# Transnormer attention and a four-expert mixture on one core: neighbouring chunks of experts 1 to 3 share two of seven up products as 256-row matmuls, down products are scaled where they lie, and the norm's factors are kept in 4 KB rows

## The chip, the cores and the metric

One Trainium2 chip, one of its cores. The time is the device time of one execution in microseconds (us). Each kernel is run several times; of the kernel before three runs are shown. A profile is one further execution, recorded by the hardware profiler.

## What is computed

The reference is an attention without softmax followed by a mixture of four experts, all in fp32:

```python
kv = np.einsum('bhsd,bhse->bhde', k, v)            # q, k, v: (8, 8, 576, 64)
out = np.einsum('bhsd,bhde->bhse', q, kv)
rms = np.sqrt(np.mean(out * out, axis=-1, keepdims=True) + 1e-06)
x = (out / rms * g_norm).transpose(0, 2, 1, 3).reshape(4608, 512)
p = domain_probs / (domain_probs.sum(-1, keepdims=True) + 1e-09)
for e in range(4):                                  # w1[e]: 512x1024, w2[e]: 1024x512
    h = np.maximum(x @ w1[e], 0.0)
    out += p[:, e:e + 1] * (h @ w2[e])
```

## The kernel before

**Tiling.** The 4608 tokens are cut into nine chunks of 512: one for each of the eight batches, and a ninth of the 64 tokens that each batch of 576 has left. The program takes the experts one after the other and, in each, all nine chunks; step `s` is expert `s // 9`, place `s % 9`. While expert 0 works on a chunk, `attention` (L1121) makes the x of the next batch. Chunks' x factors are kept in DRAM and loaded again for experts 1 to 3 (`x_again`, L1476).

**Products.** Both matrix products are done by a seven-product (Strassen-like) scheme in two levels. For the up product of a chunk there are seven outer products, taken in the order `OUTER` = (1, 2, 6, 5, 3, 7, 4), and in each of them seven inner ones, in the order `ORDER` = (1, 6, 2, 5, 7, 4, 3). One inner product of `up` (L1514) is 2 x 2 matmuls: two quarters `u` of the weights by two halves of 64 columns (`halves_of`, L581, line L585), which go to different halves of the array. A matmul is 128x64 weights by 128 moving rows of x. It shows as two records in the trace (the kernel's own `pe`, L578, counts two passes), so that an inner product is 8 records. The results lie in PSUM banks `u1`, `u2`. ScalarE (ACT) copies the result of inner product 1 into another bank as a seed, on which product 2 accumulates; it copies those of 6 and 7 to `snap` tiles, and 2 and 4 to the result tile (L1563). VectorE (DVE) adds the results of 7 and 3 to the snaps (L1571). That is five copies and two sums of 256 columns for each outer product. Sums of whole outer products follow, 128x1024 each, on DVE or GpSimd (POOL) (`combine`, L608), and ReLUs on ACT (L1527).

**Down.** `down_deep` (L1819) does the same for the down product of chunks from step 7 on, with 128 moving rows and two outer products side by side in one bank. Its results are added up (L1944), scaled by the token's probability on ACT into a separate accumulator tile (`merge`, L1716), and sent as four blocks of 128 tokens by 512 columns. Expert 0 stores them by SyncE's queue (SP), later experts add them into the output in DRAM by an accumulating DMA on POOL's queue (`send`, L1732, issued at L1740). The last chunk (`down`, L1753) loads the sum back and finishes on the core.

**The norm.** In `attention` the squares are summed on the PE, and the inverse roots of batch `b`, 64 heads-by-tokens rows of 160, are written to DRAM (`roots`, L1297) and read back broadcast over 64 partitions each (`spread`, L1306: 512 bytes a piece, two DMAs of 256 KB for each half of the chunk; `spread_left`, L1313). DVE multiplies them in (L1322, L1329) and so makes the chunk's x, from which matmuls read directly.

**What sets the order.** Nothing is written in program order. Every step adds operations with a key (the place in PE's order), an estimated cost by engine, buffers and dependencies; `Plan` (L44) is a list scheduler that plays the whole kernel through at build time and writes out one fixed order for each engine. An engine takes the operation with the earliest due time among those that are ready; SP takes the first that is ready. Kinds of buffers (`big`, 31 tiles of 128x1024; `snap`; `xf`, the five places for x factors; the PSUM banks) have a fixed number of slots and are handed out in that order. `DEALS` (L72) lists for some steps the random draws that shift due times. So any edit can move instructions everywhere; only semaphores hold at run time.

Of the kernel before, what the change touches and what calls it, by code (L numbers as in the profile page):

```python
# [43 lines left out]
class Plan:  # L44
# [410 lines left out]
def kernel(  # L455
# [68 lines left out]
        "big": (31, 2 * NT), "w1y": (7, 768), "xa": (1, 4 * NT), "xb": (1, 4 * NT),  # L524
        "w2e": (1, 2 * NT), "snap": (5, HN),
# [8 lines left out]
    for kind, n in BANKS.items():  # L534
# [16 lines left out]
    slots["w2y"] = [w2y_home[:, i, :] for i in range(3)]  # L551
    halved = slots["db"]
# [4 lines left out]
        ((kind,), "xf", [slots[kind][0][:, i * 2 * NT:(i + 1) * 2 * NT] for i in range(n)])  # L557
        for kind, n in (("xa", 2), ("xb", 2), ("w2e", 1))
# [14 lines left out]
        b: dram.tile([D, P + 32], F32, tag=f"roots{b}", name=f"roots{b}") for b in range(1, B)  # L573
# [119 lines left out]
    TAIL = (1, 6, 5, 7)  # L693
    GROUPS = ((1, 7), (6, 5), (4,))
# [426 lines left out]
    def attention(b, key, span, rem):  # L1121
# [160 lines left out]
        def invert(eng):  # L1282
# [11 lines left out]
        sent, kept_roots = Buf(None, f"root{b}"), roots[b]  # L1294
        plan.add(
            when, SPC,
            lambda eng: nc.sync.dma_start(out=kept_roots[:], in_=both[0].ap[0:P:2, 0:wide]),  # L1297
            reads=both[:1], writes=[sent], kb=41, lands=2.6,
        )
        for s, (qt, tokens, mine) in enumerate(done):  # L1300
            xh = x_halves(b)[s]

            def spread(eng, xh=xh, s=s):
                rows = kept_roots[:].rearrange("(n i s r) t -> r s i n t", i=2, s=2, r=2)
                for r in range(2):
                    nc.sync.dma_start(  # L1306
                        out=xh.ap[r * D:(r + 1) * D, :].rearrange("p (n t) -> p n t", t=P),
                        in_=rows[r, s, 0, :, 0:P].unsqueeze(0).to_broadcast([D, 8, P]))

            def spread_left(eng, s=s, mine=mine):  # L1310
                rows = kept_roots[:].rearrange("(j i s r) t -> r s i j t", i=4, s=2, r=2)
                for r in range(2):
                    nc.sync.dma_start(  # L1313
                        out=xs.ap[r * D:(r + 1) * D, mine].rearrange("p (j t) -> p j t", j=NR),
# [897 lines left out]
```

## Time and profile before

| | |
|---|---|
| median of 3 runs | 1631.18 us (1630.81 to 1631.45) |
| the profiled execution, its own time | 1631.92 us |
| its span in the trace | 1630.1 us |
| granted TensorE clock | 1.00 |
| PE / DVE / ACT / POOL busy | 1622.5 / 1337.2 / 986.9 / 612.9 us |
| moved by DMA | 241.02 MB, mean 148 GB/s |

The span leaves 1.8 us of the execution's own time outside. PE, PEld, DVE, ACT and POOL are the tensor engine's matmuls and weight loads, VectorE, ScalarE and GpSimd; SPq is SyncE, which only issues DMAs. A row of a view by lines names the line of the kernel, the engine, the operation, the tile written and the tiles read, the count, the busy time and the mean duration in ns. A row of the windows gives for a stretch of time the busy us and in brackets the number of instructions of each engine. Matmuls are pipelined: the duration of one record is a latency, and its price is the distance from start to start.

### The profile page before, as it was taken

The numbers are of one execution on the slowest core, as the hardware profiler recorded it, in microseconds if no ns is written. First come the engines' busy times: TensorE is split into PE (matmuls) and PEld (weight loads), VectorE is DVE, ScalarE is ACT, GpSimd is POOL, SyncE is SP. The second block draws the span as 40 slices with busy tenths as digits, with TensorE's granted clock in tenths as the row PEclk, the third lists the DMA queues.
The fourth block names the chain that finished last, engine by engine and source line by source line (L and its number), as shares of the span: only waits on it lengthen the run. The fifth ranks groups of instructions, "written<-read, shape, count | busy, mean of one in ns | idle before, by whom it ended". The sixth has DMA issues, their size and how long they took to land.

```text
span 1630.1 us, 66925 instructions
## 1 busy us (share of the span) xinstructions
PE 1622.5 (100%) x29082; PEld 1564.6 (96%) x29082; DVE 1337.2 (82%) x2188; ACT 986.9 (61%) x2504; POOL 612.9 (38%) x597
## 2 busy tenths in 40 slices
PE   9999999999999999999999999999999999999999
PEld 5788999989999999999999999999999999999998
DVE  5788888889888888878988888887788987777776
ACT  4456655665566666666666666666566666566563
POOL 4233432323443443344344533332344443332232
PEclk9999999999999999999999999999999999999999
DMA  9877787855664435444676454444478544444442
GB/s 242 217 190 204 204 216 194 213 166 205 183 176 125 118 93 156 119 111 113 175 190 144 107 133 114 108 111 111 131 183 184 131 107 117 118 107 117 118 106 53
DMA packets 229312, 241.02 MB, mean 148 GB/s; under 512 B 101047, under 2 KB 172542, under 8 KB 229018
## 3 DMA queue, kind: packets, MB, share of 16 engines
q1 hardware_dynamic: 205402, 199.96, 40.9%
q0 software_dynamic: 23616, 36.78, 15.2%
q8 instruction: 228, 3.74, 1.0%
q14 instruction: 66, 0.54, 0.1%
HBM read 162.21 MB, written 74.47 MB: 145 GB/s over the span
## 4 chain that ended last, share of the span: by engine, by line
PE 98%; DVE 1%; DMA 1%; ACT 0%; issue 0%; SPq 0%; DVEq 0%; ACTq 0%
PE u L585 48%; PE db L585 31%; PE ab L585 16%; PE ab L1193 1%; PE ab L1218 0%; PE ab L1261 0%; PE ab L2156 0%; PE db L1218 0%; DVE big L608 0%; DMA kv<-in_v_dram 0%; DMA out_dram<-big 0%; SPq L2079 0%; PE u L997 0%; DMA small<-in_q_dram 0%; DVE small L608 0%
## 5 line engine op out<-in xcount | busy, mean ns | idle before, releaser
L608 DVE TENSOR_TENSOR big<-big,big 128x1024 f32<-128x1024 f32 (+1 forms) x612 | 547.6, 913 | 32.3 <-ACT big L1527 14.1
L585 PE MATMUL db<-big,big 128*64 128x128 f32 (+1 forms) x5464 | 397.1, 283 | 0.3 <-DVE big L608 0.3
L585 PEld LDWEIGHTS db<-big,big 128*64 128x64 f32 x5464 | 319.1, 137 | 16.7 <-issue 0.6
L1563 ACT ACTIVATE snap<-u 128x256 f32<-128x256 f32 x490 | 187.7, 383 | 178.3 <-PE u L585 156.5
L1571 DVE TENSOR_TENSOR big<-u,snap 128x256 f32<-128x256 f32 x450 | 189.0, 421 | 112.8 <-PE u L585 74.2
L608 POOL TENSOR_TENSOR big<-big,big 128x256 f32<-128x256 f32 (+1 forms) x149 | 165.4, 1111 | 229.6 <-DVE big L608 91.0
L1563 ACT ACTIVATE big<-u 128x256 f32<-128x256 f32 x450 | 172.8, 385 | 84.1 <-PE u L585 63.5
L585 PE MATMUL u<-xb,big 128*64 128x128 f32 x2880 | 212.4, 273 | 0.1
L585 PE MATMUL u<-xa,big 128*64 128x128 f32 x2784 | 205.2, 273 | 0.1
L608 POOL TENSOR_TENSOR big<-big 128x512 f32<-128x512 f32 (+1 forms) x94 | 111.4, 1186 | 235.7 <-DVE big L608 137.4
L1905 ACT ACTIVATE snap<-db 128x256 f32<-128x256 f32 (+1 forms) x268 | 95.3, 356 | 126.8 <-PE db L585 104.4
L585 PEld LDWEIGHTS u<-xb,big 128*64 128x64 f32 x2880 | 168.8, 137 | 2.2 <-issue 0.3
L585 PE MATMUL u<-xa,w1y 128*64 128x128 f32 x2232 | 165.8, 273 | 0.0
L585 PEld LDWEIGHTS u<-xa,big 128*64 128x64 f32 x2784 | 162.5, 137 | 2.2 <-issue 1.2
L585 PE MATMUL u<-xb,w1y 128*64 128x128 f32 x2208 | 164.2, 273 | 0.0
L1527 ACT ACTIVATE big<-big 128x1024 f32<-128x1024 f32 x133 | 139.9, 1054 | 11.0 <-DVE big L608 9.4
L1913 DVE TENSOR_TENSOR big<-ab,snap 128x256 f32<-128x256 f32 x186 | 78.4, 421 | 65.6 <-ACT snap L1905 39.0
L608 DVE TENSOR_TENSOR big<-big 128x512 f32<-128x512 f32 (+1 forms) x167 | 125.2, 756 | 7.6 <-POOL big L608 4.4
L585 PEld LDWEIGHTS u<-xa,w1y 128*64 128x64 f32 x2232 | 130.6, 137 | 0.7 <-DVE xb L608 0.4
L585 PEld LDWEIGHTS u<-xb,w1y 128*64 128x64 f32 x2208 | 129.1, 137 | 1.3 <-issue 0.4
L1740 POOL DMA_DIRECT2D out_dram<-big x124 | 108.0, 1155 | 32.5 <-ACT big L1716 18.0
L1563 ACT ACTIVATE u<-u 128x256 f32<-128x256 f32 x245 | 90.9, 371 | 38.7 <-PE u L585 28.1
(246 smaller groups left out, 2838.8 us busy)
## 6 DMA issues: line engine op xcount, KB each, us to landing
xb<-x SPq DMA_DIRECT2D x44, 512.0 KB, 3.6
xa<-x SPq DMA_DIRECT2D x40, 512.0 KB, 3.6
out_dram<-big POOLq DMA_DIRECT2D x76, 256.0 KB, 6.0
big<-in_moe_w_dram SPq DMA_DIRECT2D x27, 512.0 KB, 6.3
w2e<-x SPq DMA_DIRECT2D x20, 512.0 KB, 3.6
xa<-x_h SPq DMA_DIRECT2D x37, 256.0 KB, 3.5
x_h<-big SPq DMA_DIRECT2D x18, 512.0 KB, 4.9
x<-xb SPq DMA_DIRECT2D x18, 512.0 KB, 4.9
```

The source lines that it names most:

```text
L585: nc.tensor.matmul(out_[cols], lhsT=lhsT[:, cols], rhs=rhs, **kw)
L608: lambda eng: adder(eng).tensor_tensor(out=out_(), in0=a(), in1=b(), op=op),
L1193: nc.tensor.matmul(bank.ap[o * D:(o + 1) * D, r * D:(r + 1) * D], lhsT=ks[r], rhs=vs[r], start=(j == r == 0), stop=(j == len(sets[0]) - 1) ...
L1527: lambda eng: nc.scalar.activation(out=b.ap[:], in_=b.ap[:], func=ACT.Relu),
L1563: lambda eng: nc.scalar.activation(out=where(), in_=ps.ap[:, 0:HN], func=ACT.Copy),
L1571: lambda eng: nc.vector.tensor_tensor(out=block(whole, a, t), in0=src.ap[:, 0:HN], in1=add_.ap[:], op=ALU.add),
L1740: nc.gpsimd.dma_start(out=dst, in_=cell(i)[parts, :], accum_op=ALU.add)
L1905: lambda eng: nc.scalar.activation(out=where(), in_=group_of(ps.ap), func=ACT.Copy),
L1913: lambda eng: nc.vector.tensor_tensor(out=cell(tq, dq), in0=group_of(src.ap), in1=group_of(add_.ap), op=ALU.add,),
```

## The change

Three edits and what they need around them.

1. *Shared up products* (`course`, `up_shared`, in place of `up` for experts 1 to 3). Two neighbouring chunks take two of the seven outer products together: products 7 and 4 at the end of an even place with those of the next chunk, products 2 and 3 at the end of an odd place. The five x places become one tile `x`, and the matmul's moving operand is the 128 columns of two places of it: 256 rows by the same weights. Over the three experts that is 44 joint outer products (16, 16, and 12 in expert 1, where chunk 0 is left out). In a joint product nothing is seeded in PSUM. ACT copies inner products 1, 6, 7 and 4 of both chunks to the result tiles, and DVE adds 2, 7 and 3 of both in place: eight copies and six sums for two chunks, where apart there were ten and four. The other outer products stay as they were. The order of products in a chunk becomes 2, 3, 1, 6, 5, 7, 4 or 7, 4, 1, 6, 5, 2, 3.
2. *Down finished in place* (`finish`, `places`, `down_whole`). The accumulator tiles go. ACT scales the summed product where it lies, and each of four quarters, 256 tokens by 256 columns, is sent by itself.
3. *The norm's factors*. The roots lie in DRAM so that one partition reads 4 KB in a row (512 bytes for those of the left tokens). A batch has two writes and four reads, where it had one write and eight reads.

`DEALS` is new too, and with it the order on every engine. The core of the diff, in its own order; first the tables, the x tile, the roots and the loads of x:

```diff
     DEALS = {
-        -3: (920, 388), -2: (494, 764), -1: (959, 295), 0: (983,), 3: (1126, 364), 4: (981, 960), 5:
...
+        -2: (494, 764, 127), -1: (790,), 0: (75, 333), 1: (360,), 2: (103,), 4: (998,), 5: (1064,
...
     SHAPE = {
-        "big": (31, 2 * NT), "w1y": (7, 768), "xa": (1, 4 * NT), "xb": (1, 4 * NT),
-        "w2e": (1, 2 * NT), "snap": (5, HN),
+        "big": (31, 2 * NT), "w1y": (7, 768), "snap": (5, HN),
...
+    x_home = pool.tile([P, 5, 2 * NT], F32, tag="x", name="x")
+    x_at = [x_home[:, i, :] for i in range(5)]
+    x_flat = x_home[:].rearrange("p n x -> p (n x)")
+    slots["xa"], slots["xb"] = [x_flat[:, 0:4 * NT]], [x_flat[:, 4 * NT:8 * NT]]
+    slots["w2e"] = x_at[4:]
...
     roots = {
-        b: dram.tile([D, P + 32], F32, tag=f"roots{b}", name=f"roots{b}") for b in range(1, B)
+        b: [
+            dram.tile([n, D // n, width], F32, tag=f"roots{b}_{n}", name=f"roots{b}_{n}")
+            for n, width in ((8, P), (16, 32))
+        ] for b in range(1, B)
     }
...
-        sent, kept_roots = Buf(None, f"root{b}"), roots[b]
-        plan.add(
-            when, SPC,
-            lambda eng: nc.sync.dma_start(out=kept_roots[:], in_=both[0].ap[0:P:2, 0:wide]),
-            reads=both[:1], writes=[sent], kb=41, lands=2.6,
-        )
+        sent = [Buf(None, f"root{b}_{i}") for i in range(2)]
+        for i, cols in enumerate((slice(0, P), slice(P, wide))):
+            plan.add(
+                when, SPC,
+                lambda eng, i=i, cols=cols: nc.sync.dma_start(
+                    out=roots[b][i][:].rearrange("m n t -> n m t"), in_=both[0].ap[0:P:2, cols]),
+                reads=both[:1], writes=[sent[i]], kb=(32, 8)[i], lands=2.6,
+            )
...
-            def spread(eng, xh=xh, s=s):
-                rows = kept_roots[:].rearrange("(n i s r) t -> r s i n t", i=2, s=2, r=2)
-                for r in range(2):
-                    nc.sync.dma_start(
-                        out=xh.ap[r * D:(r + 1) * D, :].rearrange("p (n t) -> p n t", t=P),
-                        in_=rows[r, s, 0, :, 0:P].unsqueeze(0).to_broadcast([D, 8, P]))
-
-            def spread_left(eng, s=s, mine=mine):
-                rows = kept_roots[:].rearrange("(j i s r) t -> r s i j t", i=4, s=2, r=2)
-                for r in range(2):
-                    nc.sync.dma_start(
-                        out=xs.ap[r * D:(r + 1) * D, mine].rearrange("p (j t) -> p j t", j=NR),
-                        in_=rows[r, s, 0, :, P:wide].unsqueeze(0).to_broadcast([D, NR, R]))
-
-            plan.add(when, {"SP": 1.2}, spread, reads=[sent], writes=[xh], kb=520, lands=6.2)
-            plan.add(when, {"SP": 1.28}, spread_left, reads=[sent], parts=[xs], kb=100, lands=6.0)
+            def spread(eng, i, to, s=s):
+                rows = roots[b][i][2 * s:2 * s + 2].rearrange("r n t -> r (n t)")
+                return nc.sync.dma_start(out=to, in_=rows.unsqueeze(1).to_broadcast([2, D, rows.shape[1]]))
+
+            plan.add(
+                when, SPC, lambda eng, xh=xh, spread=spread: spread(eng, 0, xh.ap[:, :]),
+                reads=sent[:1], writes=[xh], kb=520, lands=5.0)
+            plan.add(
+                at(4.2), SPC, lambda eng, mine=mine, spread=spread: spread(eng, 1, xs.ap[:, mine]),
+                reads=sent[1:], parts=[xs], kb=64, lands=4.5)
...
-    def x_again(c, key, step):
+    def x_again(c, keys):
         views = {}
-        for j, m in enumerate(OUTER):
+        for m, key in keys.items():
...
             views[m] = {
-                n: (f, lambda f=f, at=at: f.ap[:, at * P:(at + 1) * P])
+                n: (f, lambda f=f, at=at: f.ap[:, at * P:(at + 1) * P], at)
                 for n, at in ((1, 0), (2, 2), (3, 3), (5, 4), (7, 5), (6, 6), (4, 7))
```

The shared products:

```diff
+        for i, c in enumerate(CHUNKS[e]):
+            turn = i % 2
+            first, end = (ENDS, HEADS) if turn else (HEADS, ENDS)
+            beside = i + 1 < NCH and not (e == 1 and 0 in (c, CHUNKS[e][i + 1]))
+            todo = [m for m in OUTER if m not in shared] if not turn and not shared else [
+                m for m in first + MIDDLES[turn] + end if m not in shared]
+            joint = end[::-1] if turn else end
+            joint = joint if beside else ()
+            for m in todo:
+                if m not in joint:
+                    uses[i][m] = at, 1
+                    at += 1
+            for m in joint:
+                uses[i][m] = uses[i + 1][m] = at, 2
+                at += 2
+            shared = joint
...
+    def up_shared(s, e, i, uses, views, following):
+
+        turn, start = i % 2, e * NCH
+        made, h = pending.pop(s, {}), {}
+        after = pending[s + 1] = {}
...
+            joint = n == 2
+            name = f"{s}_{m}"
+            both = [views, following] if joint else [views]
+            wholes = [Buf("big", f"m{s + o}_{m}") for o in range(n)]
+            made[m] = wholes[0]
+            if joint:
+                after[m] = wholes[1]
+            bank = {
+                1: Buf("u1", f"u1_{name}"), 2: Buf("u2", f"u2_{name}"), 5: Buf("u2", f"u3_{name}"),
+            }
+            snap, seeds = {}, []
+            first = [{} for _ in range(n)]
...
+                def product(eng, m=m, mm=mm, ps=ps, both=both, n=n, place=place):
+                    w = w1f[e][m][mm][1]()
+                    if n == 1:
+                        x = both[0][m][mm][1]()
+                    else:
+                        lo, hi = sorted(place(0)[0])
+                        col = both[0][m][mm][2] * P
+                        x = x_home[:, lo:hi + 1:hi - lo, col:col + P]
+                    for u in range(2):
+                        halves_of(
+                            ps.ap[:, u * n * P:(u + 1) * n * P], w[:, u * P:(u + 1) * P], rhs=x,
+                            start=((mm in (1, 5) or mm == 2 and n == 2) and u == 0), stop=True,
+                            skip_group_check=True,
+                        )
+
+                op = plan.add(
+                    key, pe(2, n * P), product,
+                    reads=w1f[e][m][mm][0] + [v[m][mm][0] for v in both] + ([ps] if seeded else []),
+                    **{"parts" if seeded else "writes": [ps]},
+                    after=last[-2:-1] if mm == 1 else seeds if mm == 5 else (),
+                )
...
+                def early(o, a, t, first=first, copy=copy, cell=cell, wholes=wholes):
+                    first[o][a, t] = Buf(None, f"f{s}_{o}_{a}{t}")
+                    copy(o, wholes[o], lambda: cell(o, a, t), also=[first[o][a, t]])
+
+                if joint:
+                    for o in range(2):
+                        if mm in (1, 6, 7):
+                            early(o, *{1: (0, 0), 6: (0, 1), 7: (1, 1)}[mm])
+                        if mm == 2:
+                            total(o, 0, 0, ps, None)
+                        elif mm == 7:
+                            total(o, 1, 1, bank[5], None)
+                        elif mm == 4:
+                            copy(o, wholes[o], lambda o=o, cell=cell: cell(o, 1, 0))
+                        elif mm == 3:
+                            total(o, 0, 1, ps, None)
+                    continue
```

The end of the down product, and where the two are called:

```diff
-    def down_deep(s, e, c, groups=((1, 6), (7, 5), (4, 2), (3,)), base=None, h=None, merge=None, send=None, ends=False, sink=None):
-
-
-
-
-        mixed = h is not None
-        if not mixed:
-            h = hidden.pop(s)
-            base = s + 1.2
-            merge, send = result(s, e, c, base)
+    def down_deep(s, e, c, groups, base, h, merge=None, send=None, ends=False, sink=None, full=False):
...
+        mixed = not full
...
-            elif i == 0:
+
+    def finish(s, e, c, q, th, dh, key, prods, half, whole):
+
+        done = [Buf(None, f"of{s}_{q}_{t}") for t in range(2)]
+        for t in range(2):
+            plan.add(
+                key, act(HN),
+                lambda eng, t=t, i=2 * th + t: nc.scalar.activation(
+                    out=whole(q)[:, t * HN:(t + 1) * HN], in_=whole(q)[:, t * HN:(t + 1) * HN],
+                    func=ACT.Copy, scale=p_all[:, c * NR + i, e:e + 1]),
+                reads=[probs_later if c else probs, half[q]], writes=[done[t]],
+                holds=[prods[q][0]], after=list(half[q].readers),
+            )
+        return done
...
+        def emit(q, th, dh, key, prods, half, whole):
+            done = finish(s, e, c, q, th, dh, key, prods, half, whole)
+            where = places(c, th, dh)
+
+            def send(eng):
+                for parts, b, dst in where:
+                    src = two(whole(q))[parts, b, :]
+                    if e:
+                        nc.gpsimd.dma_start(out=dst, in_=src, accum_op=ALU.add)
+                    else:
+                        nc.sync.dma_start(out=dst, in_=src)
+
+            n = len(where)
+            plan.add(
+                key, {"POOL": 1.1 * n if n < 3 else 0.8 * n} if e else {"SP": 0.55 * n}, send,
+                reads=done + [was[2 * th + b] for b in range(2) if was[2 * th + b]],
+                parts=[now[2 * th + b] for b in range(2)], kb=256, lands=6.5 if e else 4.5,
+                holds=[prods[q][0]],
+            )
...
+                elif i == 2:
+                    add(7, 7, 4)
+                    emit(7, 1, 0, key, prods, half, whole)
+                    add(1, 1, 2)
+                    emit(1, 0, 0, key, prods, half, whole)
+                else:
+                    add(6, 6, 3)
+                    emit(6, 0, 1, key, prods, half, whole)
...
             if NCH - 2 <= s < E * NCH - 1:
-                down_deep(s, e, c)
+                down_whole(s, e, c, i % 2 if e else 0)
...
+                            m: s + 0.6 + 0.13 * j for j, m in enumerate(OUTER)})
+                    else:
...
+                        ahead = 0.4 if to == 1 and not n else 0.92
+                        x_views[s + 1] = x_again(again, {
+                            m: to * NCH + at / 7 - ahead + 0.01 * (k_ == 2 and at < 7 * (n + 1) - 0.5 and m in uses[to][n - 1] and uses[to][n - 1][m] == (at, 2) if n else 0)
+                            for m, (at, k_) in sorted(uses[to][n].items(), key=lambda t: t[1][0])})
+            if e:
+                up_shared(s, e, i, uses[e], x_views.pop(s), x_views.get(s + 1))
+            elif s:
                 up(s, e, x_views.pop(s))
```

199 lines of the change are left out of this document (176 added, 23 removed), and 7 rows, old and new, of the table DEALS.

## The prediction

> **What bounds the kernel now.** First the page: busy times, granted clock and the chain that ended last.
>
> ```profile
> span 1630.1 us, 66925 instructions
> PE 1622.5 (100%) x29082; PEld 1564.6 (96%) x29082; DVE 1337.2 (82%) x2188; ACT 986.9 (61%) x2504; POOL 612.9 (38%) x597
> PE 98%; DVE 1%; DMA 1%; ACT 0%; issue 0%; SPq 0%; DVEq 0%; ACTq 0%
> ```
>
> PE makes up 98% of the chain. A busy PE need not be at its peak, so next come the windows: four stretches of 45 us (opening, expert 0, two with the busiest DVE in experts 1 and 2), and the long steady one.
>
> ```profile
> 0.00:45.00 45.00, 43.06 (x574) 26.33 (x575) 23.87 (x63) 19.67 (x57) 18.71 (x29) 1.00 0.93 252
> 90.00:135.00 45.00, 43.45 (x770) 38.86 (x766) 38.47 (x63) 26.35 (x67) 15.08 (x13) 1.00 0.71 169
> 585.00:630.00 45.00, 45.00 (x826) 44.82 (x824) 41.04 (x67) 28.92 (x75) 18.85 (x24) 1.00 0.46 122
> 855.00:900.00 45.00, 45.00 (x828) 45.00 (x826) 40.74 (x75) 27.92 (x71) 21.76 (x24) 1.00 0.66 150
> 945.00:1575.00 630.00, 630.00 (x11546) 629.90 (x11544) 509.55 (x811) 392.14 (x997) 230.21 (x221) 1.00 0.50 125
> ```
>
> In experts 1 to 3 PE never idles: 630 us for 11546 records of 128 rows is 54.6 ns each, at full clock. Only the opening, which the change leaves as it is but for its order, and expert 0 have holes, in expert 0 most in 90 to 135, 1.55 us. Which waits those are, after the opening:
>
> ```profile
> PE u L585 <- DMA small<-in_q_dram: 1.2, 1, 1.2
> PE db L585 <- DVE big L608: 0.3, 1, 0.3
> PE ab L1193 <- DMA out_dram<-big: 0.2, 1, 0.2
> ```
>
> So there are two things to gain: PE records that cost less, and 1.7 us of waits, nearly all one wait.
>
> **Shared up products: what PE saves.** 44 joint outer products have 7 inner ones of 8 records with 256 rows, 2464 records, in place of 4928 with 128. The trace has 128x256 matmuls in the last chunk and 128x512 ones in the opening. Starts of the PE timeline:
>
> ```profile
> 1610.98 1.90 PE L585 MATMUL u<-big,big 128*64 128x256 f32 x16
> 1612.70 1.04 PE L585 MATMUL db<-big,big 128*64 128x128 f32 x16
> 1614.89 1.90 PE L585 MATMUL u<-big,big 128*64 128x256 f32 x16
> 1616.61 0.61 PE L585 MATMUL db<-w2y,big 128*64 128x128 f32 x8
> 1618.36 1.90 PE L585 MATMUL db<-big,big 128*64 128x256 f32 x16
> 1620.09 0.61 PE L585 MATMUL db<-small,big 128*64 128x128 f32 x8
> ```
>
> And two pieces of the chain, both of 128x512 matmuls:
>
> ```profile
> 25.99 8.73 PE u L585 x40
> 37.97 4.29 PE u L585 x20
> ```
>
> From start to start, 16 records of 256 rows take 1.72, 1.72 and 1.73 us, 107.7 ns each; two records of 128 take 2 x 54.6 = 109.2. Each record that disappears saves 1.5 ns. From 512 rows: 4.29/20 = 214.5 ns against 4 x 54.6 = 218.4, 1.3 ns for each of three that disappear; 8.73/40 = 218.3 saves nothing. So the saving lies between 0 and 1.5 ns; I take 1.3, for the starts are rounded to 10 ns and the 20 records agree with them to that. 2464 x 1.3 = 3.2 us (0 to 3.7). No row shows moving rows in two pieces of 128 columns; if every piece were paid like a matmul of its own, the gain would be the lower end, 0. A cost above that would need more than the records it replaces, which no row suggests.
>
> The Trainium skill ("TensorE: Matmul & The Clock Gate", "Wait — 56ns, not 53.3ns?") states a fixed cost of about 2.5 ns for each matmul on top of its rows; by that, 2464 fewer would save 6.2 us. The rows here halve it.
>
> **What the evacuation gains and loses.** Rows by line and shape:
>
> ```profile
> L1563 ACT ACTIVATE u<-u 128x256 f32<-128x256 f32 x245 | 90.9, 371 | 38.7 <-PE u L585 28.1 <-DVE big L1571 0.7
> L1571 DVE TENSOR_TENSOR big<-u,snap 128x256 f32<-128x256 f32 x450 | 189.0, 421 | 112.8 <-PE u L585 74.2 <-ACT snap L1563 32.0 <-PE db L585 1.4
> L1716 ACT ACTIVATE big<-big,p_all 128x256 f32<-128x256 f32 x196 | 91.1, 501 | 2.0 <-DVE big L1944 1.0 <-POOL big L1944 0.7
> L1740 POOL DMA_DIRECT2D out_dram<-big x124 | 108.0, 1155 | 32.5 <-ACT big L1716 18.0 <-ACT snap L1563 5.4 <-ACT u L1563 3.9
> L719 POOL DMA_DIRECT2D big<-in_moe_w_dram x17 | 22.0, 1295 | 17.1 <-ACT snap L1563 11.7 <-issue 2.7 <-ACT big L1563 1.6
> ```
>
> Each joint product has two copies fewer and two sums more. ACT loses 88 x 371 ns = 33 us, DVE gains 88 x 421 ns = 37 us, 1.4 us in each 45 us of experts 1 to 3. The busiest window shown has DVE at 41.04 of 45, so it would stand at 42.4: PE's 45 still cover it. The order also moves 18 of the 1024-wide sums from DVE to POOL, which is idle 62% of the time. A bank is now held for two copies (0.74 us) while PE fills another for 0.86 us (8 x 107.7 ns), where it was 0.37 us against 0.44: the same proportion. I take 0.
>
> On PE, in expert 1, this is how it looks. `u` are banks of up products, `ab` and `db` of down products between them; before:
>
> ```order
> L585 MATMUL u_122<-xb_111,big_88 64x128 x4
> L585 MATMUL ab_128<-big_93,big_97 64x128 x4
> L585 MATMUL ab_128<-big_102,big_91 64x128 x4
> L585 MATMUL u_123<-xa_110,w1y_108 64x128 x4
> L585 MATMUL ab_129<-w2y,big_74 64x128 x4
> L585 MATMUL ab_129<-w2y,big_81 64x128 x4
> L585 MATMUL u_125<-xb_111,w1y_106 64x128 x4
> ```
>
> And in the change, the same engine and expert, in a joint product:
>
> ```order
> L592 MATMUL u_119<-x,w1y_107 64x256 x4
> L592 MATMUL db_124<-big_75,big_97 64x128 x4
> L592 MATMUL db_124<-big_72,big_85 64x128 x4
> L592 MATMUL u_121<-x,big_84 64x256 x4
> L592 MATMUL db_124<-w2y,big_81 64x128 x4
> L592 MATMUL db_124<-small,big_91 64x128 x4
> L592 MATMUL u_122<-x,w1y_107 64x256 x4
> ```
>
> A row of four 256-wide matmuls (8 records) stands between two rows of four down matmuls: the down product still covers each evacuation.
>
> The x loads are as many and as large, and their five places are the same; a joint product keeps two of them for 7 x 0.86 us = 6 us plus the down matmuls between. From issue to landing (the page's list of DMA issues) they take 3.6 us, so they stay hidden; uncovered, one late load would cost PE up to that.
>
> ```profile
> xa<-x SPq DMA_DIRECT2D x40, 512.0 KB, 3.6
> out_dram<-big POOLq DMA_DIRECT2D x76, 256.0 KB, 6.0
> big<-in_moe_w_dram POOLq DMA_DIRECT2D x17, 512.0 KB, 7.9
> big<-roots SPq DMA_DIRECT2D x28, 256.0 KB, 4.9
> ```
>
> **Down finished in place.** The scalings stay: the order has 224 of them before and after, 501 ns on an ACT that is 61% busy. POOL issues 152 DMAs instead of 128; at 1155 ns, or 1295 as for the weights with their 1 KB rows, that is 28 to 31 us on POOL, hidden in its idle 62%. The pieces have 1 KB rows instead of 2 KB, so a DMA may land after 7.9 us instead of 6.0; it keeps the product's tile 1.9 us longer, against which two accumulator tiles a chunk become free. 0.
>
> **The norm's factors.** The long wait of expert 0, seen on SP, DVE and PE:
>
> ```profile
> 105.67 0.48 SPq L1297 DMA_DIRECT2D roots<-big  x1
> 109.35 2.24 SPq L1306 DMA_DIRECT2D big<-roots  x2
> 111.68 1.24 SPq L1313 DMA_DIRECT2D snap<-roots  x2
> 113.01 1.25 SPq L1306 DMA_DIRECT2D big<-roots  x2
> 120.06 1.29 DVE L1322 SCALAR_TENSOR_TENSOR big<-small,gcol,big 128x1024 f32<-128x1024 f32 x1 [1.61 <-DMA big<-roots]
> 121.40 0.66 PE L585 MATMUL u<-big,big 128*64 128x128 f32 x8 [1.20 <-DMA small<-in_q_dram]
> ```
>
> The second half's factors were issued 3.66 us after the first's; they land at 120.0, DVE multiplies until 121.35, and 0.05 us later PE starts on that x. The row of PE names a load of q, but its own start follows DVE's end: the wait is for the factors. SP's rows at that place (`roots` written, `big` the factors of a half, `snap` those of left tokens), before:
>
> ```order
> L1297 DMA roots_216<-big_82 64x160
> L2079 DMA out_dram<-big_79 64x256 x4
> L1306 DMA big_82<-roots_216 64x8x128 x2
> L1313 DMA snap_114<-roots_216 64x4x32 x2
> L1306 DMA big_102<-roots_216 64x8x128 x2
> L1313 DMA snap_114<-roots_216 64x4x32 x2
> L2079 DMA out_dram<-big_93 64x256 x4
> ```
>
> And in the change:
>
> ```order
> L1308 DMA roots_8_215<-big_82 8x8x128
> L1308 DMA roots_16_216<-big_82 4x16x32
> L621 DMA kv<-in_k_dram 120x2x256
> L1317 DMA big_95<-roots_8_215 128x1x1024
> L1317 DMA big_82<-roots_8_215 128x1x1024
> L1317 DMA snap_114<-roots_16_216 128x1x128 x2
> L2364 DMA out_dram<-big_75 64x256 x4
> ```
>
> The second half now follows the first by one issue, about 0.6 us (1.25/2), not 3.66. A half is one DMA of 512 KB; as x loads of that size and row it should land in 3.6 us rather than 4.9. Together that is over 3 us earlier, against 1.2 us of wait; the additional write of roots takes back 0.5 us. So the 1.2 us go. What could be late next are the k and v loads that stand behind the `roots` on SP's queue: there are fewer issues ahead of them, so they gain too. I take 1.2 us (0, if the new order puts another wait there; up to 1.7 with the two small ones).
>
> **The sum.** 3.2 + 1.2 = 4.4 us off the profiled execution's own 1631.92 us (span 1630.1 and 1.8 outside it): 1627.5. It ran 0.7 us above the median; off the median, 1631.2 - 4.4 = 1626.8 us.
>
> **The rivals.** *The records alone* (22%): the new order makes as large a wait in expert 0, where SP's queue is still a row of issues with hardly a break. For it: a change of any operation reorders all. 1631.2 - 3.2 = 1628.0.
>
> *All holes close* (9%): beside the records the whole of 90 to 135 is filled (1.55 us) and what PE lost behind shorter stalls in expert 0, about as much again: 1631.2 - 3.2 - 3.1 = 1624.9.
>
> *Nothing* (9%): pieces of 128 moving columns are paid like separate records and only one wait moves: about 1630.5, within 0.2%.
>
> *Slower* (7%): DVE takes PE's place. Its 88 more sums bunch in pairs at the joint products, and DVE's load at the starts of experts (41 of 45) leaves no room. It decides where a joint product's six sums (2.5 us) come later than the next use of their banks, in 6 us of PE time for two products in flight. Slower by 0.2% begins at 4.4 + 3.3 = 7.7 us, one fifth of the 37 us not hidden; with a third it is 12.3 - 4.4 = 7.9 us on top: 1639. Against it: DVE's own waits are for PE (74.2 us in the row of L1571), so it waits for results, not the reverse.
>
> *Weight loads bound PE* (1%): PEld is busy 629.90 of 630 us in the long window. If the 54.6 ns were the load of 64 columns, half the loads in joint products would save 2464 x 54.6 ns = 135 us, to 1497. Against it: 512-row records cost 3.9 times those of 128, so rows set the time, not loads. The Trainium skill has such a rule ("TensorE: Matmul & The Clock Gate", "Back-to-back issue gap": 81 ns at 128 rows, 131 at 512 in a stream with weight loads); the trace here disagrees, with 54.6 and 214.5.
>
> **How the numbers follow.** The forecast has 52%. 0.2% is 3.3 us, about what a measurement of this kernel can tell from no change: faster means under 1627.9. The forecast lies 1.1 us under that: nine tenths of it (0.47), the closing of all holes (0.09), the weight loads (0.01) and 0.03 of the records alone, which lie 0.1 us over the line, make 0.60. The rest of these two (0.05 and 0.19) and nothing (0.09) make 0.33. Slower has 0.07. The range goes from 1624.0, below the closing of all holes, to 1630.6, so that the nothing case is in; outside it lie slower, and the tails.
>
> **What would show it.** Right: joint rows 128x256 of `u<-x` at 215 ns for two records; PE 45.00 of 45 in experts 1 to 3; no PE wait over 1 us in 90 to 135; DVE at most 43 of 45. Wrong: PE waits for DVE's in-place sums or for ACT's copies out of `u`, or PE idle for SP's loads in expert 0, or 256-row records at 109 ns.

## The result and the profile after

The change makes the kernel slower: 1740.26 us, the median of 4 runs (1739.28 to 1741.39), against 1631.32 us of the kernel before in 4 runs (1630.81 to 1631.77). The ratio is 1.0668, with a 95% interval of 1.065 to 1.0687. The forecast was 1626.8 us. The profiled execution took 1739.79 us, its span 1738.0.

From the page of the kernel after, the span, the busy times, the granted clock in 40 slices of 43 us and the chain that ended last:

```profile
span 1738.0 us, 61711 instructions
PE 1649.4 (95%) x26618; PEld 1506.2 (87%) x26618; DVE 1313.4 (76%) x2252; ACT 942.8 (54%) x2416; POOL 703.1 (40%) x645
PEclk9898898899899999999999999999999999999999
PE 85%; DMA 11%; DVE 2%; SPq 1%; ACT 1%; issue 0%; DVEq 0%; ACTq 0%
```

PE falls from 98% of the chain to 85%, and DMA has 11%, where it had 1%. The clock falls short only in the first third. So the windows of the kernel after are split where expert 0 has made its last x:

```profile
45.00:500.00 455.00, 372.62 (x6010) 332.83 (x6010) 281.25 (x457) 202.46 (x519) 123.39 (x113) 0.89 0.53 154
945.00:1575.00 630.00, 630.00 (x10080) 579.35 (x10078) 520.84 (x899) 368.90 (x945) 290.08 (x264) 1.00 0.55 129
```

The same two stretches of the kernel before are shown next (the second stands in the prediction, 630.00 of 630):

```profile
45.00:500.00 455.00, 453.04 (x7972) 415.77 (x7970) 383.97 (x637) 271.64 (x690) 157.59 (x143) 1.00 0.71 195
```

In experts 1 to 3 PE still has no gap. In 45 to 500 us it idles 82.4 us instead of 2.0, and its mean clock there is 0.89. The waits of the kernel after, by what ended them (us in total, times, longest), name the cause:

```profile
PE u L592 <- DVE big L1595: 42.1, 8, 15.1
PE u L592 <- DVE big L1328: 39.9, 7, 7.3
DVE big L1328 <- DMA big<-roots: 106.4, 14, 9.9
```

These are two of PE's rows and one of DVE's. L1328 is DVE's multiplication by the norm's factors. There are 14 of them, two for each of seven batches, and every one waits for the DMA that reads the factors, 7.6 us on average. PE then waits for L1328, or for L1595, which stands behind it on DVE. The last batch, by the timeline of the kernel after, first SP's queue:

```profile
441.21 1.16 SPq L1317 DMA_DIRECT2D big<-roots  x2
442.42 17.78 SPq L1317 DMA_DIRECT2D snap<-roots  x2
460.30 4.04 SPq L2358 DMA_DIRECT2D out_dram<-big  x2
```

then DVE's rows, and below the dots PE's, from the same timeline (in brackets the idle time before the row and what ended it):

```profile
453.94 1.28 DVE L1328 SCALAR_TENSOR_TENSOR big<-small,gcol,big 128x1024 f32<-128x1024 f32 x1 [7.37 <-DMA big<-roots]
464.11 1.28 DVE L1328 SCALAR_TENSOR_TENSOR big<-small,gcol,big 128x1024 f32<-128x1024 f32 x1 [8.89 <-DMA big<-roots]
...
450.63 0.64 PE L592 MATMUL u<-x,big 128*64 128x128 f32 x8
466.38 1.98 PE L592 MATMUL u<-x,w1y 128*64 128x128 f32 x16 [15.11 <-DVE big L1595]
```

The two halves' DMAs are issued together at 441.21. DVE can start on the first half 12.7 us later and on the second 10.2 us after that, and PE stands still for 15.1 us. What the DMA engines do meanwhile shows in the last two columns of the windows (mean busy share of the 16 DMA engines, GB/s), and the granted clock in the column before them:

```profile
452.00:460.00 8.00, 0.00 (x0) 0.00 (x0) 1.28 (x1) 0.00 (x0) 0.00 (x0) 0.58 0.13 52
455.00:460.00 5.00, 0.00 (x0) 0.00 (x0) 0.22 (x1) 0.00 (x0) 0.00 (x0) 0.50 0.13 52
```

A share of 0.13 is that of two engines of sixteen (0.125). In the kernel before, at the place where it reads its factors, the share is 0.70:

```profile
110.00:115.00 5.00, 5.00 (x114) 5.00 (x112) 3.84 (x10) 2.67 (x8) 1.47 (x2) 1.00 0.70 139
```

A half of 512 KB at 52 GB/s takes 10.1 us, which is the distance between the two halves. SP is held for 17.78 us at the DMAs that it issues behind them, so the next stores of its queue, at 460.30, are late as well.

The granted clock falls to 0.50 during such a wait and stays there for some time behind it. In the last batch that is from 453.29 to 470.36, and the 38 records of PE in that stretch take 3.98 us, 105 ns each, where records of 128 rows took 54.6 ns in the kernel before. There are eleven such stretches up to 471 us, 95.6 us together, and PE is busy in 52.1 us of them.

### The profile page after: what moved, and what is told of

It reads as the page before. It is cut to its first block, busy times and chain, and to the rows that moved or that the text cites. A ratio compares the mean times of both kernels' runs of the same rounds, so it can differ in the third digit from the quotient of the medians.

```text
span 1738.0 us, 61711 instructions
## 1 busy us (share of the span) xinstructions
PE 1649.4 (95%) x26618; PEld 1506.2 (87%) x26618; DVE 1313.4 (76%) x2252; ACT 942.8 (54%) x2416; POOL 703.1 (40%) x645
## 4 chain that ended last, share of the span: by engine, by line
PE 85%; DMA 11%; DVE 2%; SPq 1%; ACT 1%; issue 0%; DVEq 0%; ACTq 0%
PE u L592 42%; PE db L592 26%; PE ab L592 15%; DMA big<-roots 8%; SPq L621 1%; PE ab L1203 1%; DMA big<-in_v_dram 1%; DMA roots<-big 1%; DVE big L1328 1%; DMA big<-in_k_dram 0%; DMA small<-in_q_dram 0%; PE ab L1228 0%; DMA out_dram<-big 0%; DVE big L615 0%; PE ab L1271 0%
## 5 line engine op out<-in xcount | busy, mean ns | idle before, releaser
L592 PE MATMUL u<-x,big 128*64 128x128 f32 (+1 forms) x5216 | 456.7, 301 | 0.0
L592 PE MATMUL u<-x,w1y 128*64 128x128 f32 (+1 forms) x4248 | 382.6, 303 | 41.4 <-DVE big L1595 41.2
L592 PEld LDWEIGHTS u<-x,big 128*64 128x64 f32 x5216 | 325.4, 138 | 27.5 <-issue 1.9
L592 PEld LDWEIGHTS u<-x,w1y 128*64 128x64 f32 x4248 | 268.1, 139 | 69.9 <-DVE big L1595 43.1
L2229 POOL DMA_DIRECT2D out_dram<-big x140 | 149.8, 1536 | 94.9 <-ACT big L2191 45.9
L1791 DVE TENSOR_TENSOR big<-u,big 128x256 f32<-128x256 f32 x249 | 94.9, 418 | 56.0 <-PE u L592 42.1
L1781 ACT ACTIVATE snap<-u 128x256 f32<-128x256 f32 x202 | 77.4, 383 | 75.5 <-PE u L592 65.1
L1791 DVE TENSOR_TENSOR big<-u,snap 128x256 f32<-128x256 f32 x190 | 80.1, 422 | 48.7 <-PE u L592 27.7
L1661 ACT ACTIVATE big<-big 128x1024 f32<-128x1024 f32 x102 | 107.6, 1056 | 11.9 <-DVE big L615 11.3
L592 PE MATMUL ab<-w2y,big 128*64 128x128 f32 x1576 | 112.9, 276 | 0.0
L592 PE MATMUL u<-big,big 128*64 128x128 f32 (+2 forms) x552 | 67.3, 376 | 39.9 <-DVE big L1328 39.9
L592 PEld LDWEIGHTS ab<-w2y,big 128*64 128x64 f32 x1576 | 94.5, 139 | 4.5
L1328 DVE SCALAR_TENSOR_TENSOR big<-small,gcol,big 128x1024 f32<-128x1024 f32 x14 | 18.0, 1284 | 106.4 <-DMA big<-roots 106.4
```

Source lines behind the costliest of these rows:

```text
L592: nc.tensor.matmul(out_[cols], lhsT=lhsT[:, cols], rhs=rhs, **kw)
L1328: lambda eng, xh=xh, qt=qt: nc.vector.scalar_tensor_tensor(out=two(xh.ap[:]), in0=tokens(qt.ap, False), scalar=gcol[:], in1=two(xh.ap[:]), ...
L1661: lambda eng: nc.scalar.activation(out=to.ap[:], in_=to.ap[:], func=ACT.Relu),
L1781: lambda eng: nc.scalar.activation(out=where(), in_=rows(o, ps), func=ACT.Copy),
L1791: lambda eng: nc.vector.tensor_tensor(out=cell(o, a, t), in0=rows(o, src), in1=own[0].ap[:].rearrange("p (u t) -> p u t", t=P) if own else ...
L2229: nc.gpsimd.dma_start(out=dst, in_=src, accum_op=ALU.add)
```

## The experiments

**The theory.** The new read of the factors is written as [2, 64, 1024] on the DRAM side: two rows, each repeated 64 times, 4 KB in one piece. In the kernel before each DMA had the 64 copies outermost. The theory is that the outermost dimension of 2 puts the whole DMA on two engines. The Trainium skill ("DMA: Bandwidth & Descriptors", "Why a DMA increments its semaphore by 16 and not by 1", the paragraph on how many engines) has this rule: the number of engines is the largest one up to 16 that divides the slowest dimension of both sides. For 2 and 128 that is 2, and the share of 0.13 agrees. The rivals are that one DMA instead of two is what is slow, that the issue on SP's queue is, or that the new order and the other parts of the change bring the loss.

**two_dmas.** Each half is read by two DMAs, the 64 copies outermost; nothing else changes, the order included.

```diff
-                return nc.sync.dma_start(out=to, in_=rows.unsqueeze(1).to_broadcast([2, D, rows.shape[1]]))
+                for r in range(2):
+                    nc.sync.dma_start(
+                        out=to[r * D:(r + 1) * D, :], in_=rows[r].unsqueeze(0).to_broadcast([D, rows.shape[1]]))
```

> The change, with each half's factors read by two DMAs of 64 partitions instead of one of 128; rows of 4 KB, bytes and the order on all engines stay. Theory (a read whose outermost pattern has 2 rows runs on two of the sixteen DMA engines; the after profile shows DMA share 0.13, that is 2/16, and 52 GB/s while it waits): the outermost pattern is now 64, the halves land in 5 us or less instead of 11.6 and 21.7 us, DVE's wait for the factors falls from 106.4 us to under 10, and the time comes to the prediction's 1626.8 us (1624 to 1631). Rival 1 (all readers fetch the same few DRAM rows, which limits the rate whatever the number of engines): 52 GB/s stays, 1735 to 1745 us. Rival 2 (the new order in expert 0 or the shared products, not the reads): 1735 to 1745 us too, with the waits elsewhere.

Measured: 1630.09 us (11 runs) against 1630.49 (15 runs) of the kernel before, ratio 0.9996 (0.9987 to 1.0005). The whole loss is gone with this one edit. DVE's timeline for the first such batch of two_dmas:

```profile
61.11 1.28 DVE L1330 SCALAR_TENSOR_TENSOR big<-small,gcol,big 128x1024 f32<-128x1024 f32 x1
62.91 1.28 DVE L1330 SCALAR_TENSOR_TENSOR big<-small,gcol,big 128x1024 f32<-128x1024 f32 x1 [0.52 <-DMA snap<-roots]
```

The waits of 7 to 9 us are gone. The window of 45 to 500 us of two_dmas, where PE idles 1.3 us:

```profile
45.00:500.00 455.00, 453.74 (x7840) 413.60 (x7840) 378.60 (x618) 268.57 (x682) 170.74 (x159) 1.00 0.70 194
```

But the 4.4 us of the forecast are not there either; the later runs ask why.

**two_dmas_k2 and two_dmas_k4.** As two_dmas, with as many DMAs, bytes and rows, but the 64 copies written as 2 x 32 or as 4 x 16 (the edit with 4 is shown):

```diff
-                        out=to[r * D:(r + 1) * D, :], in_=rows[r].unsqueeze(0).to_broadcast([D, rows.shape[1]]))
+                        out=to[r * D:(r + 1) * D, :],
+                        in_=rows[r].unsqueeze(0).unsqueeze(0).to_broadcast([4, D // 4, rows.shape[1]]))
```

> As two_dmas, but each DMA's source pattern is 2 x 32 rows of 4 KB. Theory: two engines again, DMA share 0.13, time as the change, 1735 to 1750 us, although there are two DMAs a half as in two_dmas. Rival 3 (how many DMAs, not how many engines): 1627 us.

> As two_dmas, but each DMA's source pattern is written as 4 x 16 rows of 4 KB instead of 64 (same bytes, same places). Theory: four engines, DMA share about 0.25 and about 105 GB/s in the waits, a half in 5 us; the factors' landings come 5 and 10 us earlier than in the change, so that of 106 us of DVE's wait some 30 to 45 are left and the time lies between, 1645 to 1680 us. Rival 1 (rows): as two_dmas, whatever that gives. Rival 3 (how many DMAs, not how many engines): 1627.

Measured, one run each: 1747.42 us with 2, as expected, and 1680.24 with 4, just above the 1645 to 1680 that were expected. The DMA share during the first such batch, in the windows of two_dmas_k2 and then of two_dmas_k4:

```profile
64.00:68.00 4.00, 0.00 (x0) 0.00 (x0) 0.00 (x0) 0.00 (x0) 0.00 (x0) 0.68 0.13 52
```

```profile
64.00:68.00 4.00, 0.00 (x0) 0.00 (x0) 1.17 (x1) 0.00 (x0) 0.00 (x0) 0.80 0.25 99
```

The share is 2/16 and 4/16, the rate about doubles with it (52 and 99 GB/s), and the time follows. Two DMAs instead of one change nothing by themselves: with 2 outermost the loss is back in full. That settles the cause.

**before_new_roots and before_two_dmas.** The kernel before with the third edit alone, the reads as in the change, or split as in two_dmas. Each gets an order of its own from the scheduler.

> The kernel before with the edit of the norm's factors alone (its order comes out anew). Theory: the whole loss comes with this edit: 14 waits of DVE for the factors, 90 to 115 us in all, 1715 to 1750 us. Rival 2 (shared products or in-place down make the loss): 1628 to 1633 us.

> The kernel before with the new norm code alone, its reads split so that each DMA's outermost dimension is the 64 copies. Theory: no loss is left (before_new_roots lost 130 us), and the 1.2 us wait for the factors in 110 to 122 us goes or moves elsewhere: 1629.3 to 1631.5. Rival 1: 4 KB rows are worth the 1.2 us forecast: 1629.3. Rival 2: the two writes of roots and SP's new order cost expert 0 a wait of their own: 1632.5 to 1635.

Measured: 1760.78 us (one run), 11 us above the range of the theory, so the loss needs no joint products and no scaling in place. With the split 1648.88 us (4 runs), ratio 1.0104 (1.0089 to 1.012): 112 us of it go, but the result is 18 us slower than the kernel before, which neither the theory nor its rivals gave. DVE waits only 1.6 us for the factors in it, so the reads themselves are not late; more on these 18 us below.

**small_factors_k2.** two_dmas, with only the left tokens' factors (64 KB, 512-byte rows) read by one DMA again:

```diff
+                if i:
+                    return nc.sync.dma_start(out=to, in_=rows.unsqueeze(1).to_broadcast([2, D, rows.shape[1]]))
                 for r in range(2):
```

> two_dmas, but the factors of the left tokens (64 KB, 512-byte rows) are read again by one DMA whose outermost dimension is 2. Theory (such a DMA runs on two engines, 64 rows each; the time goes by bytes and rows): a DMA of 512-byte rows is over in 4 to 6 us and is not waited for, so 1630 to 1640; the big factors carry nearly all of the loss. Rival (the issue on SP's queue is what is slow, whatever the size): SP stands still at these reads for 8 us or more and k and v come late, 1660 to 1740.

Measured: 1631.72 us, one run. SP's row in the first such batch, in small_factors_k2:

```profile
59.56 1.20 SPq L1318 DMA_DIRECT2D snap<-roots  x2
```

Two issues of the same form take 1.2 us here and 17.86 in the first such batch of the change. The form is not slow to issue. SP is held by what was issued in front of it: in the same batch the four issues for the left tokens' factors take 16.28 us in two_dmas_k2, 6.30 in two_dmas_k4 and 3.19 in two_dmas.

**old_norm_code and no_joint.** The change with the norm's code of the kernel before, and two_dmas without joint products (`beside = False`). Both give the scheduler other operations, so it finds another order.

> The changed kernel with the norm's factors written and read as in the kernel before (512-byte pieces); the joint products and the down product finished in place stay. Theory: the joint records are worth 3.2 us (1.32 ns for each of 2464), the new norm code even over all 16 queues' engines gives nothing, so this is within 1 us of two_dmas: 1629 to 1631. Rival: the new norm code costs expert 0 some 2 to 3 us in any form, which ate the gain of the joint records in two_dmas: then this runs at 1626.5 to 1628, 3 us under the kernel before.

> two_dmas with no joint up products: every outer product by itself, with 128 moving rows, in the new order. Theory: the joint records' 3.2 us stand in the end time, since PE has no hole in experts 1 to 3: 1633.3, 3.2 us over two_dmas' 1630.1. Rival: PE has a limit beside the records (evacuation, a clock), and joint and single products end together: within 0.8 us of 1630.1.

Measured: 1639.94 us, ratio 1.0054 (1.0042 to 1.0067), and 1640.32 us, ratio 1.0056 (1.0043 to 1.0069), 5 runs each. Both lose 10 us against two_dmas, more than either theory or rival allowed. A run in which the order moves does not measure the part that was taken out. The next four keep the order or change nothing else.

**no_draws.** two_dmas with `DEALS` empty: the same operations, another order. Beside it **two_dmas_again** as the reference.

> two_dmas with the table of draws empty: the same operations and sizes, another order on every engine. Theory (old_norm_code, no_joint and before_two_dmas lost 9 to 18 us by an order that fits them less, not by what they compute): this loses as much, 1636 to 1655, in many stalls under 2 us. Rival (their losses come from the operations they took back): within 3 us of two_dmas, 1627 to 1633.

> two_dmas once more, as the reference for the three kernels beside it, which keep its order or its operations. All theories: 1629.5 to 1630.7, 0 to 1 us under the kernel before.

Measured: 1639.26 us, ratio 1.005 (1.0038 to 1.0063), and 1630.21 us (11 runs) against 1631.05 (21 runs) of the kernel before, ratio 0.9996 (0.9987 to 1.0005). The order alone is worth 9.1 us. PE in the window of expert 0, of no_draws and then of two_dmas_again:

```profile
45.00:500.00 455.00, 449.05 (x7748) 404.51 (x7744) 366.80 (x617) 265.89 (x675) 176.39 (x145) 1.00 0.69 192
```

```profile
45.00:500.00 455.00, 453.67 (x7816) 413.07 (x7816) 376.98 (x618) 267.65 (x681) 170.57 (x159) 1.00 0.69 193
```

PE idles 6.0 us there instead of 1.3, in many short stalls; its longest wait in no_draws is 2.3 us. The additional idle time is 4.6 of the 9.1 us; the rest was not placed. So an order alone can cost what old_norm_code and no_joint lost, and half of the 18 us of before_two_dmas. That the order is the cause in these three is likely, but not shown: each also has other operations.

**joint_as_singles.** two_dmas in its own order; each joint matmul of 256 rows is issued as two of 128 into the same columns.

```diff
-                            ps.ap[:, u * n * P:(u + 1) * n * P], w[:, u * P:(u + 1) * P], rhs=x,
...
+                        for j in range(n):
+                            halves_of(
+                                ps.ap[:, (u * n + j) * P:(u * n + j + 1) * P], w[:, u * P:(u + 1) * P],
+                                rhs=x if n == 1 else x[:, j, :],
```

> two_dmas in its own order on every engine, but each joint 256-row matmul is issued as two of 128 rows in the same place, into the same columns of the same bank. Theory: the record's price is all that differs, 2464 x 1.32 ns = 3.2 us: 1633.0 to 1633.6. Rival 1: pairs of 128 rows with one weight load between them lie hidden, 1630 (within 0.8 us). Rival 2: the 10.2 us that no_joint lost were the work of joint records, and come back here: 1638 to 1641.

Measured: 1632.82 us (11 runs), ratio 1.0012 (1.0003 to 1.0022), beside 1630.21 of two_dmas_again: 2.6 us by the medians, and 2.9 by the spans of the profiled executions (1632.0 and 1629.1). That is a little under the 3.2 of the first term and of the theory, and within the term's bounds of 0 to 3.7; neither rival fits.

**factors_512.** two_dmas in its own order, but the roots laid out so that a partition reads its 4 KB in eight pieces of 512 bytes, and the left tokens' 512 bytes in four of 128.

```diff
-            dram.tile([n, D // n, width], F32, tag=f"roots{b}_{n}", name=f"roots{b}_{n}")
+            dram.tile([D, width], F32, tag=f"roots{b}_{n}", name=f"roots{b}_{n}")
...
-                rows = roots[b][i][2 * s:2 * s + 2].rearrange("r n t -> r (n t)")
+                rows = roots[b][i][:].rearrange("(n i s r) t -> r s i n t", i=(2, 4)[i], s=2, r=2)
```

> two_dmas in its own order, but the roots are laid out as in the kernel before, so that a partition reads its 4 KB in eight pieces of 512 bytes; as many DMAs, as many bytes, over the same 64 copies. Theory: the row's length is worth next to nothing (4.8 us to landing in two_dmas, 4.9 in the kernel before): within 0.7 us of two_dmas. Rival (the forecast's step: longer rows land 1.3 us earlier, and PE waits for the factors once): 1.2 us more than two_dmas.

Measured: 1641.51 us (5 runs), ratio 1.0066 (1.0053 to 1.0079), 11.3 us over two_dmas_again. Both the theory then held and the rival were far off. From the DMA issues of factors_512 and of two_dmas_again (count, KB, median us from issue to landing):

```profile
big<-roots SPq DMA_DIRECT2D x28, 256.0 KB, 7.0
```

```profile
big<-roots SPq DMA_DIRECT2D x28, 256.0 KB, 5.0
```

In one and the same order, rows of 4 KB land 2.0 us earlier. Short pieces alone don't make the 7.0: old_norm_code also reads pieces of 512 bytes, in another order, and they land in 4.8 us. PE's waits for the norm's multiplication, or for the DVE work behind it, are 9.4 us in factors_512 and 0.8 in two_dmas_again; the rows of factors_512:

```profile
PE u L592 <- DVE big L1599: 5.8, 6, 2.1
PE u L592 <- DVE big L1332: 3.6, 3, 1.6
```

**before_order_4k.** The last question was whether the forecast's second term exists in the order of the kernel before. Its order is kept on every engine; only the roots are laid out as in the change, by two writes, and each read stays two DMAs with the 64 copies outermost.

> The kernel before in its own order on every engine, but the roots laid out as in the change (two writes, 4 KB in a row for the big factors, 512 bytes for the left tokens' ones), each read still two DMAs whose outermost dimension is the 64 copies. The forecast's second term by itself: 0.7 to 1.2 us under the kernel before, with the wait at 120 us gone. Theory after factors_512 (a landing is 2 us earlier with 4 KB rows than with 512-byte ones in the same order): the same, 1.0 us under, or up to 2 where stalls of DVE hang on it. Rival: this order was already fitted to late factors and the seven more issues on SP cost as much, so within 0.4 us of the kernel before.

Measured: 1630.76 us (11 runs) against 1631.2 (15 runs), ratio 0.9998 (0.9989 to 1.0007). The profiled span is 1629.0, 1.1 us under that of the kernel before. The landing, the multiplication that was late, and the window around it, from the DMA issues, DVE's timeline and the windows of before_order_4k:

```profile
big<-roots SPq DMA_DIRECT2D x28, 256.0 KB, 4.0
```

```profile
118.27 1.28 DVE L1329 SCALAR_TENSOR_TENSOR big<-small,gcol,big 128x1024 f32<-128x1024 f32 x1 [0.35 <-DMA big<-roots]
```

```profile
90.00:135.00 45.00, 44.66 (x796) 40.40 (x794) 39.91 (x65) 27.69 (x71) 16.56 (x14) 1.00 0.71 184
```

The factors land in 4.0 us instead of 4.9, the second multiplication starts at 118.27 instead of 120.06, and PE's wait at 121.40 is gone: 44.66 us busy of 45, where it had 43.45. The trace shows the 1.2 us of the second term at this place; the medians, 0.4 us apart, can't tell it from nothing, and so don't decide between theory and rival.

## Why the prediction was wrong, point by point

- **The bound** was right: PE sets the end, and whatever stops PE is paid in full.
- **The joint records** were right in mechanism and size. The timeline of the kernel after, in expert 2, start to start:

```profile
1356.37 1.05 PE L592 MATMUL u<-x,big 128*64 128x256 f32 x8
1357.24 0.63 PE L592 MATMUL db<-w2y,big 128*64 128x128 f32 x8
1357.67 0.63 PE L592 MATMUL db<-small,big 128*64 128x128 f32 x8
1358.11 1.05 PE L592 MATMUL u<-x,w1y 128*64 128x256 f32 x8
1358.97 1.06 PE L592 MATMUL ab<-big,big 128*64 128x128 f32 x16
```

  8 records of 256 rows take 0.87 and 0.86 us, 108 ns each, as the rows of the last chunk had said; joint_as_singles measures 2.6 us for all of them, where 3.2 was forecast. The 6.2 us that the Trainium skill ("TensorE: Matmul & The Clock Gate", "Wait — 56ns, not 53.3ns?") would give by its fixed 2.5 ns for each matmul do not show here. Two places of x in one moving operand cost no more than one.
- **The evacuation** at 0 was right: PE has no gap in experts 1 to 3, and DVE has 520.84 of 630 us there, 37 of 45. DVE's whole load did not rise by 37 us but fell from 1337.2 to 1313.4. The 18 of the 1024-wide sums that went to POOL are a part of that; the rest was not taken apart. POOL's load rose from 612.9 to 703.1, by these sums and by its DMA issues.
- **Down finished in place** at 0 shows no wait of PE for its transfers, but it was not tried by itself. POOL's issues cost more than the 1155 to 1295 ns of the forecast, 1536, and still lay hidden; the 256 KB output DMAs land in 5.6 us, under the 7.9 that were allowed. A row of the groups of the kernel after, and one of its DMA issues:

```profile
L2229 POOL DMA_DIRECT2D out_dram<-big x140 | 149.8, 1536 | 94.9 <-ACT big L2191 45.9 <-ACT big L1781 10.2 <-DVE big L615 7.3
```

```profile
out_dram<-big POOLq DMA_DIRECT2D x72, 256.0 KB, 5.6
```

- **The norm's factors**: here is the step that failed, "A half is one DMA of 512 KB; as x loads of that size and row it should land in 3.6 us rather than 4.9." It compared DMAs by size and row and left out the shape. An x load has 128 partitions outermost on both sides; this read has 2 on the DRAM side. It ran on 2 of 16 engines at 52 GB/s, and a half took 10.1 us of them, the second waiting for the first. What was costed at a gain of 1.2 us cost 110: 1740.26 us with these reads, 1630.09 with the same order and split reads. The two traces, after and two_dmas, have the same 26618 records of PE, and their spans are 110.4 us apart. Of these, 81.7 us are idle time of PE (88.6 against 6.9) and 28.7 us are longer records (1649.4 us busy against 1620.7). The clock gives most of the latter: half of the 52.1 us that PE is busy at 0.50 is 26 us.
- **The rivals** all missed it. The one on the slower side put the mishap on DVE in experts 1 to 3. The profile could not show the new form, but both numbers for a bound were there: the diff's [2, 64, 1024], and the Trainium skill's table ("DMA: Bandwidth & Descriptors", "Rules for kernel authors"), which says that a small outermost dimension confines a DMA to that many engines. With it, an estimate was at hand: in 110 to 115 us of the kernel before, the DMAs move 139 GB/s at a share of 0.70, so two engines at that pace move 25 GB/s, and a half of 512 KB takes 21 us. It took 10.1, and both are far beyond a wait of 1.2 us. The same table advises one 128-partition transfer instead of two to its halves; here the merged transfer is the slow one, 1740.26 us, and the two halves 1630.09.
- **The sum without that fault**: two_dmas is 0.4 us under the kernel before, and 0.8 in the second measurement, not 4.4. The records' gain is shown in its order (joint_as_singles), and the longer rows are worth 11.3 us there (factors_512). But before_order_4k shows that the order of the kernel before paid about 1 us at most for its short rows. The new order is another one, and no_draws shows that orders of these operations can lie 9 us apart. The forecast reckoned with the new order only as one more wait in expert 0. About 2 us of the records' gain are given back. It is not in one wait: PE's idle time hardly moved (7.6 us before, 6.9 and 7.0 in the two profiles of these reads), but its busy time fell by 1.8 and 0.4 us (1622.5 to 1620.7 and 1622.1), not by 3.2. Where the records cost more stays open, and the intervals of the runs (2.1 us under to 0.8 over) are as wide as the effect. Even the rival of the records alone, 3.2 us under, promised more than was measured.

## What to carry to other kernels

Before a DMA's landing is taken from a row of the same size, compare the outermost dimension of both its sides as well: a broadcast of two rows in one DMA has a 2 there, and merging two DMAs into one can be what brings it. In the windows the fault shows at once, as a DMA share that stands at a small multiple of 1/16 while engines wait. And where a scheduler makes the order, test a part by an edit that keeps the order; one that changes it measures the order too, 9 us here.

## What the runs showed of the hardware that was not expected

- With an outermost dimension of 2, 4 and 64 the share of the DMA engines was 0.13, 0.25 and 0.86 (the last in two_dmas, 56 to 62 us, with what else ran there); 52 GB/s on two engines is 26 GB/s each, with 4 KB rows one row in 159 ns (64 rows of an engine in 10.2 us).
- SP is held when it issues behind such a backlog, 17.78 us for two small DMAs that take 1.2 us to issue otherwise. So a DMA that is slow on two engines also delays the transfers that stand behind it on the issuing queue.
- After some microseconds without work PE's granted clock was 0.50 (the window of 455 to 460 us; PE's last group of records had begun at 450.63). The Trainium skill ("TensorE: Matmul & The Clock Gate", "What's actually happening") says that an idle window halves the clock, and the trace agrees. So a wait was paid once as idle time and again as slower records behind it: 81.7 and 28.7 us here.
- With 512-byte pieces instead of 4 KB rows, over all engines, a read of 256 KB took 7.0 us instead of 5.0 in one order and 4.9 instead of 4.0 in another. The order moved it as much: 512-byte pieces landed in 4.8 us in old_norm_code, 4 KB rows in 4.9 in no_draws.
